# A third store buffer and separate scratch for the squares in the experts' weight conversion of a retention and expert-routing kernel

## The chip, the cores and the metric

The kernel runs on one core of a Trainium2 chip. The core has TensorE for matmuls (with weight loads that the profile lists apart as PEld), VectorE (DVE), ScalarE (ACT), GpSimd (POOL), and SyncE (SP), whose queue issues nearly all DMAs here. The metric is the device time of one execution in microseconds (us), lower being better.

## What is computed

Three layers follow one another on 3072 tokens of width 512. Inputs and outputs are float32.

```python
# retention: per batch and head
state = gamma * state + outer(k[t], v[t])
y[t]  = q[t] @ state / sqrt(D)
# dense layer, d_ff = 2048, with a PReLU
h = x @ w_in
x = (max(h, 0) + alpha * min(h, 0)) @ w_out
# experts: 8 of them, each w1[e] 512x1024 and w2[e] 1024x512, one chosen per token
expert_idx = argmax(normalise(x) @ normalise(expert_emb).T / tau)
out[mask_e] = gate_w[mask_e] * (max(x[mask_e] @ w1[e], 0) @ w2[e])
```

## The kernel before

**Halves.** The large matmuls run on pairs of float16 numbers. A float32 matrix is multiplied by a power of two, its rounded value is the high half, and what is left is the low half; a product then takes three float16 matmuls. `split` does it for a piece of 128x1024: ScalarE writes the high half (an activation with a scale) and VectorE the low half (one scalar_tensor_tensor).

**Order of the work.** Everything is first recorded by a planner (`Plan`) and then issued. The planner knows which instruction reads or writes which bytes of which buffer, adds assumed durations, and from both makes one fixed order for each engine's queue. TensorE's instructions are only put in when their operands are due 1.5 us earlier by its reckoning (`MARGIN`). On the chip each queue runs in that order, and an instruction that must wait holds up all that stand behind it on its engine. A buffer that is free earlier therefore changes two things: what must be waited for, and where the planner puts the instructions.

**The dense layer.** The tokens are taken in 6 blocks of 512. For each block there are 16 steps, 96 in all. A step is `mm1` (12 matmuls of 512 columns into a PSUM bank), then a Relu on ScalarE and three more instructions on ScalarE and VectorE, by which the bank is freed and the halves for the next matmul are made, then `mm2` (12 matmuls). `mm1` is written 2 steps ahead (`LA = 2`). The weights' halves lie in `win` and `wout`, of which 16 chunks of 512 float32 hold the halves; each has two more chunks behind them (`KF + 2`), because the raw weights are read in two chunks further on and shrink forward. These two chunks hold nothing once the dense weights are split. Retention of later tokens and the routing of finished blocks lie between the steps.

**The experts' weights.** While the dense layer runs, the experts' 16 matrices (here called halves 0 to 15, `HALVES`) are read, turned into float16 pairs and written to DRAM (`wsplit`), from where each is loaded when its expert is due. Each goes through in 4 pieces of 128x1024:

- `half_load` reads a piece from DRAM into one of 6 buffers in `stage`.
- `half_scale` lets ScalarE square and sum the 4 pieces (`square_sum`, whose elementwise result goes to scratch and is never read), then a TensorE matmul, `total`, adds the sums over the partitions, and VectorE derives the scale.
- `half_pair` splits a piece into one of the buffers of `out_ring`, stores that to DRAM from SyncE's queue, and reads the piece that is six further on into the buffer that became free.

Before, `out_ring` has two buffers, the last four of `stage`'s 16 float16 chunks, and the squares write their scratch into the same two.

Of the kernel before, what the change touches and what calls it, by code (L numbers as in the profile page):

```python
# [10 lines left out]
F16 = mybir.dt.float16  # L11
# [17 lines left out]
KF = DFF // P  # L29
# [296 lines left out]
def retention_prelu_moe_kernel(ctx: ExitStack, tc, qkv, w_in, w_out, alpha, emb, tau, w1, w2,  # L326
# [14 lines left out]
    def buf(name, shape, dt=F32):  # L341
        return sbuf.tile([P, *shape], dt, name=name, tag=name)
# [12 lines left out]
    def tmp(name, shape, dt=F32, n=2):  # L355
        if name not in small:
            small[name] = Ring([buf(f"{name}_{k}", shape, dt) for k in range(n)])
        return small[name].next()
# [17 lines left out]
    win = buf("win", [KF + 2, 512])  # L376
    wout = buf("wout", [KF + 2, 512])
# [24 lines left out]
    stage16 = stage.rearrange("p c x -> p (c x)").bitcast(F16).rearrange("p (k a x) -> p k a x", k=16, a=2)  # L402
# [22 lines left out]
    def pow2(ss, s, c, hb=None):  # L425

        if hb is None:
            hb = tmp(f"hb{ss.shape[1]}", [ss.shape[1]], I32)
        V.tensor_scalar(out=hb, in0=ss.bitcast(I32), scalar1=0x7F000000, scalar2=1,
                        op0=ALU.bitwise_and, op1=ALU.logical_shift_right)  # L430
        V.tensor_scalar(out=s.bitcast(I32), in0=hb, scalar1=-1, scalar2=c << 23, op0=ALU.mult, op1=ALU.add)
        return hb

    def pow2_inverse(hb, i, c):
        V.tensor_scalar(out=i.bitcast(I32), in0=hb, scalar1=(254 - c) << 23, scalar2=None, op0=ALU.add)

    def total(acc, n):

        ps = m_ring.next()
        T.matmul(out=ps[:, 0:n], lhsT=ones32, rhs=acc, start=True, stop=True)  # L440
        t = tmp("tot", [1])
        V.tensor_reduce(out=t, in_=ps[:, 0:n], axis=AX.X, op=ALU.add)
        return t

    def square_sum(src, acc, junk):
        A.activation(out=junk, in_=src, func=AF.Square, accum_out=acc)
# [268 lines left out]
    iwe = [buf(f"iwe{g}", [E]) for g in range(2)]  # L715
    HALVES = [(e, which) for e in range(E - 1, -1, -1) for which in range(2)]
    raw_ring = Ring([stage[:, 2 * k:2 * k + 2, :].rearrange("p c x -> p (c x)") for k in range(6)])
    out_ring = Ring([stage16[:, 2 * k:2 * k + 2] for k in (6, 7)])
    half_t = {}

    def half_load(p):
# [7 lines left out]
    def half_scale(n):  # L729
        e, which = HALVES[n]  # L730
        acc = tmp("acce", [4])
        for g in range(4):
            square_sum(half_t[n, g], acc[:, g:g + 1], out_ring.bufs[g % 2][:, :, 0, :])
        s = tmp("se", [1])
        c = (C_W1, C_WIDE)[which]
        pow2_inverse(pow2(total(acc, 4), s, c), iwe[which][:, e:e + 1], c)
        half_t[n] = s
# [152 lines left out]
    acc = {}  # L890
# [120 lines left out]
    for i in range(2 * B, NTILE):  # L1011
        c, b = divmod(i, B)
        s = KF * (c - 1) + 3 * b
        early = i < first_late
        if not early:
            k = 2 + int((i - first_late) * 4.5)
            early = k < KF * (c - 2) + 14
            k = min(k, s)
# [9 lines left out]
    for n in range(len(HALVES)):  # L1028
        s = KF + BT + 4 * n
        at(s, half_scale, n)  # L1030
        for g in range(4):
            at(s + 1 + g, half_pair, n, g)
# [4 lines left out]
    for s in range(NS + BT + 12):  # L1037
# [5 lines left out]
        for o in range(BT - 1, -1, -1):  # L1043
            n = s - o
            if n >= NS - KF:
                n = max(s - LAG[o], NS - KF - 1)
# [286 lines left out]
```

## Time and profile before

| what | value |
|---|---|
| median of 3 runs | 1017.08 us |
| lowest and highest | 1011.92 and 1018.13 us |
| the profiled execution's own time | 1014.34 us |
| its span in the profile | 1012.6 us |
| granted TensorE clock, mean over the span | 0.967 of full speed |

The profiled execution is one of its own, 1.7 us longer than the span that the rows below cover, and 2.7 us under the median of the three timed runs. A row's time is measured from the start of the span. "Idle before" is time in which an engine did nothing, put down to what released it last. Nearly all instructions have the line L146, because the planner issues them from one place; the names of the buffers tell them apart. Squares are the rows `stage<-stage`, the scaling activations `stage<-stage,se`, the `total` matmuls `bank<-acce,cst`, reads of raw pieces `stage<-in_w`, stores `wsplit<-stage`.

### The profile page before, as it was taken

The numbers are of one execution on the slowest core, as the hardware profiler recorded it, in microseconds if no ns is written. First come the engines' busy times: TensorE is split into PE (matmuls) and PEld (weight loads), VectorE is DVE, ScalarE is ACT, GpSimd is POOL, SyncE is SP. The second block draws the span as 40 slices with busy tenths as digits, with TensorE's granted clock in tenths as the row PEclk, the third lists the DMA queues.
The fourth block names the chain that finished last, engine by engine and source line by source line (L and its number), as shares of the span: only waits on it lengthen the run. The fifth ranks groups of instructions, "written<-read, shape, count | busy, mean of one in ns | idle before, by whom it ended". The sixth has DMA issues, their size and how long they took to land. (4 is left out here: it accounts for less than half of the span.)

```text
span 1012.6 us, 18929 instructions
## 1 busy us (share of the span) xinstructions
PE 929.1 (92%) x7100; PEld 558.5 (55%) x7100; DVE 569.1 (56%) x1477; ACT 466.2 (46%) x825; POOL 93.3 (9%) x110
## 2 busy tenths in 40 slices
PE   5797889999998999999999899999599999988995
PEld 5774555555544544444444344446476776765763
DVE  4889988488766866686556448638422221221231
ACT  2568865385767777686565557322011010110100
POOL 0000000000100020001000200111311211232010
PEclk9798879999999999999999999999799999999998
DMA  8988623547789866766676655687564599634760
GB/s 298 303 255 268 221 97 112 177 115 196 253 231 231 201 228 221 218 209 209 197 208 187 209 166 161 237 322 176 136 194 115 141 308 319 174 95 114 165 269 23
DMA packets 129823, 201.44 MB, mean 199 GB/s; under 512 B 89726, under 2 KB 90110, under 8 KB 124608
## 3 DMA queue, kind: packets, MB, share of 16 engines
q1 hardware_dynamic: 123168, 179.42, 59.8%
q0 software_dynamic: 6560, 20.77, 6.0%
q8 instruction: 57, 0.93, 0.4%
q14 instruction: 38, 0.31, 0.1%
HBM read 204.59 MB, written 51.14 MB: 253 GB/s over the span
## 5 line engine op out<-in xcount | busy, mean ns | idle before, releaser
L146 PE MATMUL bank<-xT,win 128*128 128x512 f16 (+1 forms) x2208 | 335.5, 308 | 19.9 <-DMA xT<-f_buf 9.4
L146 PEld LDWEIGHTS <-win 128*128 128x128 f16 x2400 | 186.0, 99 | 158.2 <-issue 30.8
L146 PE MATMUL bank<-wout,f_buf 128*128 128x512 f16 x960 | 223.2, 379 | 3.9 <-DVE pay_buf L146 2.8
L146 PEld LDWEIGHTS <-f_buf 128*128 128x128 f16 x960 | 92.2, 99 | 109.3 <-issue 5.8
L146 DVE SCALAR_TENSOR_TENSOR stage<-stage,se 128x1024 f16<-128x1024 f32 x64 | 81.4, 1284 | 40.8 <-ACT stage L146 36.2
L146 DVE SCALAR_TENSOR_TENSOR g<-g,oma,bank 128x512 f32<-128x512 f32 x96 | 71.0, 742 | 41.9 <-ACT g L146 41.5
L146 ACT ACTIVATE st_bd<-bank 128x512 f16<-128x512 f32 x30 | 17.9, 597 | 156.9 <-PE bank L146 121.0
L146 ACT ACTIVATE stage<-stage,se 128x1024 f16<-128x1024 f32 x64 | 71.8, 1142 | 34.1 <-DMA wsplit<-stage 30.9
L146 ACT ACTIVATE stage<-stage 128x1024 f16<-128x1024 f32 x64 | 67.4, 1054 | 34.9 <-DMA wsplit<-stage 30.4
L146 ACT ACTIVATE g<-bank 128x512 f32<-128x512 f32 x96 | 56.2, 588 | 52.5 <-PE bank L146 51.1
L146 DVE SCALAR_TENSOR_TENSOR f_buf<-g,f_buf 128x512 f16<-128x512 f32 x80 | 55.0, 687 | 38.7 <-ACT f_buf L146 37.0
L146 POOL DMA_INDIRECT table<-pay_buf,rposi x24 | 26.2, 1092 | 500.6 <-DVE csum L146 138.0
L146 PEld LDWEIGHTS <-wout 128*128 128x128 f16 x1152 | 65.5, 98 | 7.9 <-issue 5.0
L146 PE MATMUL bank<-xT,wout 128*128 128x128 f16 x1056 | 62.6, 219 | 3.7 <-issue 3.6
L146 ACT ACTIVATE f_buf<-g 128x512 f16<-128x512 f32 x80 | 49.8, 622 | 33.0 <-DVE g L146 32.9
L146 PEld LDWEIGHTS <-st_bd 128*128 128x128 f16 x408 | 39.7, 99 | 45.4 <-issue 1.9
L146 DVE SCALAR_TENSOR_TENSOR st_bd<-bank,st_bd 128x512 f16<-128x512 f32 x34 | 23.5, 690 | 67.1 <-ACT st_bd L146 67.0
L146 DVE TENSOR_SCALAR xT<-bank,f_buf,cqk_sb 128x512 f32<-128x512 f32 x22 | 17.8, 809 | 67.1 <-PE bank L146 67.0
L146 PE MATMUL bank<-win,st_bd 128*128 128x512 f16 x216 | 49.5, 387 | 0.0
L146 POOL DMA_INDIRECT out<-xT,ids x25 | 25.3, 1011 | 217.0 <-DVE xT L146 184.1
L146 PE MATMUL bank<-wout,stage 128*128 128x512 f16 (+1 forms) x200 | 44.6, 375 | 0.0
L146 PE MATMUL bank<-wout,st_bd 128*128 128x512 f16 x192 | 42.7, 379 | 0.0
(249 smaller groups left out, 1129.8 us busy)
## 6 DMA issues: line engine op xcount, KB each, us to landing
win<-wsplit SPq DMA_DIRECT2D x56, 1024.0 KB
wout<-wsplit SPq DMA_DIRECT2D x52, 1024.0 KB
stage<-in_w SPq DMA_DIRECT2D x64, 512.0 KB
wsplit<-stage SPq DMA_DIRECT2D x64, 512.0 KB
qk_buf<-in_qkv SPq DMA_DIRECT2D x15, 768.0 KB
f_buf<-in_w_in SPq DMA_DIRECT2D x12, 512.0 KB
vp_buf<-in_qkv SPq DMA_DIRECT2D x20, 256.0 KB
f_buf<-in_w_out SPq DMA_DIRECT2D x10, 512.0 KB
```

What stands on the lines that cost most here:

```text
L146: call = lambda: fn(**kw)
```

## The change

The third buffer of `out_ring` is the space of two chunks behind `win`'s halves. The squares' scratch moves to the two chunks behind `wout`'s halves, which are cut into two buffers that take turns. The squares no longer touch a buffer that is stored.

```diff
     raw_ring = Ring([stage[:, 2 * k:2 * k + 2, :].rearrange("p c x -> p (c x)") for k in range(6)])
-    out_ring = Ring([stage16[:, 2 * k:2 * k + 2] for k in (6, 7)])
+
+    tail = [w[:, KF:KF + 2].rearrange("p c x -> p (c x)").bitcast(F16) for w in (win, wout)]
+    out_ring = Ring([stage16[:, 2 * k:2 * k + 2] for k in (6, 7)] + [tail[0].rearrange("p (c a x) -> p c a x", c=2, a=2)])
+    junk_ring = Ring([tail[1][:, 1024 * k:1024 * k + 1024].rearrange("p (c x) -> p c x", c=2) for k in range(2)])
     half_t = {}
...
         for g in range(4):
-            square_sum(half_t[n, g], acc[:, g:g + 1], out_ring.bufs[g % 2][:, :, 0, :])
+            square_sum(half_t[n, g], acc[:, g:g + 1], junk_ring.next())
```

No computation is added or taken away. The planner's order changes from the first squares on. Three places follow.

ScalarE, around half 13 (its squares are the rows with `acce_174`; `g_86` and `g_87` are the Relus of the dense steps, `se_175` and `se_176` the scales of the halves before it and of its own). Before:

```order
L146 ACTIVATE stage<-stage,se_175 128x2x512 [waits DMAHW5_49,Activation_49]
L146 ACTIVATE g_87<-bank_94 128x512 [waits DVE_49,PE_49]
L146 ACTIVATE stage,acce_174<-stage 128x2x512 [waits DMAHW7_49,DMAHW6_49]
L146 ACTIVATE stage,acce_174<-stage 128x2x512 [waits DMAHW3_49,Activation_49]
L146 ACTIVATE f_buf<-g_87 128x512 [waits DVE_49]
L146 ACTIVATE stage,acce_174<-stage 128x2x512 [waits DMAHW1_49,DMAHW0_49]
L146 ACTIVATE stage,acce_174<-stage 128x2x512 [waits DMAHW4_49,Activation_49]
L146 ACTIVATE g_86<-bank_93 128x512 [waits PE_49]
L146 ACTIVATE f_buf<-g_86 128x512 [waits DVE_49]
L146 ACTIVATE stage<-stage,se_176 128x2x512 [waits DVE_49]
```

After, in the same place of the work:

```order
L146 ACTIVATE wout,acce_174<-stage 128x1024 [waits DMAHW4_49]
L146 ACTIVATE g_87<-bank_94 128x512 [waits PE_49]
L146 ACTIVATE f_buf<-g_87 128x512 [waits DVE_49]
L146 ACTIVATE wout,acce_174<-stage 128x1024 [waits DMAHW7_49,Activation_49]
L146 ACTIVATE stage<-stage,se_175 128x2x512 [waits DMAHW3_49,DVE_49]
L146 ACTIVATE stage<-stage,se_175 128x2x512 [waits DMAHW5_49]
L146 ACTIVATE g_86<-bank_93 128x512 [waits PE_49,Activation_49]
L146 ACTIVATE win<-stage,se_175 128x2x512 [waits DMAHW0_49]
L146 ACTIVATE f_buf<-g_86 128x512 [waits DVE_49]
L146 ACTIVATE stage<-stage,se_175 128x2x512 [waits DMAHW2_49,Activation_49]
L146 ACTIVATE g_87<-bank_94 128x512 [waits PE_49]
L146 ACTIVATE wout,acce_174<-stage 128x1024 [waits DMAHW3_49]
```

Before, the four squares stand together behind all four scalings of the half before, and two of them have two DMA waits each, one for a piece to arrive and one for a store to end. After, the first two stand ahead of those scalings, and each waits for its piece alone. Over the whole order the last square of half 13 stands behind 76 Relus before and behind 72 after, and its `total` on TensorE behind 77 and 74 `mm1` steps.

ScalarE, where the first squares come in (`ssx`, `ssa`, `spv`, `syv` belong to retention), the difference:

```order
 L146 ACTIVATE v_103<-vp_buf,spv_155 128x512
 L146 ACTIVATE st_y<-st_bd,syv_160 128x512
+L146 ACTIVATE wout,acce_173<-stage 128x1024 [waits DMAHW3_49,DVE_49]
+L146 ACTIVATE wout,acce_173<-stage 128x1024 [waits DMAHW4_49]
 L146 ACTIVATE xh,ssx_130<-bank_95 128x512 [waits DMAHW7_49,PE_49]
 L146 ACTIVATE v_103,ssa_154<-vp_buf 128x512 [waits DMAHW0_49,DVE_49]
 L146 ACTIVATE xh<-bank_95,sx_132 128x512 [waits DVE_49,Activation_49]
 L146 ACTIVATE f_buf<-g_86 128x512
+L146 ACTIVATE wout,acce_173<-stage 128x1024 [waits DMAHW6_49]
 L146 ACTIVATE p_0_101,ssa_154<-vp_buf 128x512 [waits DVE_49]
 L146 ACTIVATE p_1_102,ssa_154<-vp_buf 128x512 [waits DVE_49]
+L146 ACTIVATE wout,acce_173<-stage 128x1024 [waits DMAHW1_49]
```

The squares of half 0 move ahead by some 28 rows, to where retention has ScalarE nearly to itself.

SyncE's queue, around the pieces of half 12 (stores `wsplit`, reads `stage<-in_w`). Before:

```order
L146 DMA wsplit<-stage 128x2048 [waits DMAHW2_49,DVE_49]
L146 DMA stage<-in_w 128x1024 [waits DMAHW3_49]
L146 DMA stage<-in_w 128x1024 [waits DMAHW4_49,DVE_49]
L146 DMA wsplit<-stage 128x2048 [waits DMAHW5_49]
L146 DMA stage<-in_w 128x1024 [waits DMAHW6_49,DVE_49]
L146 DMA wsplit<-stage 128x2048 [waits DMAHW7_49]
```

After:

```order
L146 DMA wsplit<-stage 128x2048 [waits DMAHW2_49,DVE_49]
L146 DMA stage<-in_w 128x1024 [waits DMAHW3_49]
L146 DMA stage<-in_w 128x1024 [waits DMAHW4_49,DVE_49,Activation_49]
L146 DMA wsplit<-win 128x2048 [waits DMAHW5_49]
L146 DMA stage<-in_w 128x1024 [waits DMAHW6_49,DVE_49,Activation_49]
L146 DMA stage<-in_w 128x1024 [waits DMAHW7_49,DVE_49,Activation_49]
L146 DMA wsplit<-win 128x2048 [waits DMAHW0_49]
```

The third store of a half now stands behind the read that needs the fourth piece to be split. TensorE's rows that wait for a DMA are 205 before and after.

## Rows read from the trace of the kernel before

**Rows 1.** The page: busy time, share and instructions of each engine.

```profile
PE 929.1 (92%) x7100; PEld 558.5 (55%) x7100; DVE 569.1 (56%) x1477; ACT 466.2 (46%) x825; POOL 93.3 (9%) x110
```

**Rows 2.** Windows, the stage of the experts' halves; columns as named.

```profile
core 0: us, PE busy (x) PEld busy (x) DVE busy (x) ACT busy (x) POOL busy (x), PEclk, DMA share, GB/s
...
196.00:620.00 424.00, 401.72 (x2400) 200.80 (x2399) 284.67 (x730) 288.23 (x530) 24.79 (x32) 0.99 0.69 205
```

**Rows 3.** Windows of 25 us within that stage, the same columns.

```profile
200.00:225.00 25.00, 25.00 (x185) 14.89 (x184) 19.28 (x49) 20.30 (x43) 0.00 (x0) 1.00 0.45 117
...
325.00:350.00 25.00, 21.78 (x150) 11.64 (x149) 20.18 (x73) 19.74 (x35) 0.00 (x0) 1.00 0.86 185
...
425.00:450.00 25.00, 22.35 (x152) 11.70 (x152) 19.88 (x58) 20.30 (x40) 0.00 (x0) 1.00 0.75 218
```

**Rows 4.** Waits, whole span: us in total, times, longest us.

```profile
ACT stage L146 <- DMA wsplit<-stage: 61.3, 42, 3.9
...
PE bank L146 <- ACT stage L146: 11.7, 10, 3.6
PE bank L146 <- DMA xT<-f_buf: 9.4, 1, 9.4
```

**Rows 5.** Timeline of TensorE: start, duration, instruction [idle before it].

```profile
286.47 0.39 PE L146 MATMUL bank<-acce,cst 128*128 128x4 f32 x2 [1.50 <-ACT stage L146]
...
313.20 0.39 PE L146 MATMUL bank<-acce,cst 128*128 128x4 f32 x2 [1.55 <-DVE rhb L146]
329.80 0.81 PE L146 MATMUL bank<-wout,f_buf 128*128 128x512 f16 x3 [2.39 <-DVE pay_buf L146]
...
370.43 0.39 PE L146 MATMUL bank<-acce,cst 128*128 128x4 f32 x2 [1.83 <-ACT stage L146]
...
424.89 0.39 PE L146 MATMUL bank<-acce,cst 128*128 128x4 f32 x2 [0.62 <-ACT stage L146]
```

**Rows 6.** Timeline around the `total` of half 13.

```profile
576.61 1.06 ACT L146 ACTIVATE stage<-stage 128x1024 f16<-128x1024 f32 x1 [3.12 <-DMA wsplit<-stage]
...
578.99 0.59 PE L146 MATMUL bank<-acce,cst 128*128 128x4 f32 x2 [3.57 <-ACT stage L146]
...
579.44 5.28 PE L146 MATMUL bank<-xT,win 128*128 128x512 f16 x12
...
587.21 2.75 PE L146 MATMUL bank<-xT,win 128*128 128x512 f16 x12
```

**Rows 7.** Windows of 5 us behind it, columns as in rows 2.

```profile
580.00:585.00 5.00, 5.00 (x14) 1.76 (x12) 3.81 (x8) 2.95 (x4) 0.45 (x1) 0.53 0.21 79
595.00:600.00 5.00, 5.00 (x25) 2.29 (x24) 1.44 (x2) 3.41 (x6) 0.00 (x0) 1.00 0.68 216
```

**Rows 8.** Timeline of one piece: scaled, split, stored, and who waits for the store.

```profile
384.97 1.15 ACT L146 ACTIVATE stage<-stage,se 128x1024 f16<-128x1024 f32 x1 [2.31 <-DMA wsplit<-stage]
...
386.15 1.28 DVE L146 SCALAR_TENSOR_TENSOR stage<-stage,se 128x1024 f16<-128x1024 f32 x1 [2.36 <-ACT stage L146]
...
387.46 0.33 SPq L146 DMA_DIRECT2D stage<-in_w  x1
387.84 0.42 SPq L146 DMA_DIRECT2D wsplit<-stage  x1
...
390.95 1.06 ACT L146 ACTIVATE stage<-stage 128x1024 f16<-128x1024 f32 x1 [3.13 <-DMA wsplit<-stage]
```

**Rows 9.** The page, costliest groups: busy us, mean ns | idle before, releaser.

```profile
L146 ACT ACTIVATE stage<-stage,se 128x1024 f16<-128x1024 f32 x64 | 71.8, 1142 | 34.1 <-DMA wsplit<-stage 30.9
L146 ACT ACTIVATE stage<-stage 128x1024 f16<-128x1024 f32 x64 | 67.4, 1054 | 34.9 <-DMA wsplit<-stage 30.4
```

**Rows 10.** Timeline where half 0's fourth square now stands, SyncE's queue and ScalarE.

```profile
182.12 0.33 SPq L146 DMA_DIRECT2D stage<-in_w  x1
...
183.24 0.19 ACT L146 ACTIVATION_READ_ACCUMULATOR p<-vp_buf 128x1 f32 x1
185.85 1.33 ACT L146 ACTIVATE p<-vp_buf,spv 128x512 f16<-128x512 f32 x2 [2.42 <-DVE spv L146]
```

## The prediction, made before the changed kernel ran

> **What bounds the kernel now.** I read the page first. TensorE is busy 92% of the span, ScalarE 46% [rows 1], so a wait of ScalarE is worth only what TensorE loses by it. Then the table of waits: ScalarE waits 61.3 us, 42 times, for stores of the experts' halves, while TensorE waits 11.7 us, 10 times, for a ScalarE write to `stage` [rows 4]. The windows limit the rest: from 196 to 620 us, where the halves are made, TensorE is busy 401.72 of 424 us [rows 2]. The reader should see 61 us of waiting on an engine with slack, and 424.00 - 401.72 = 22.3 us of idle time on the one that counts. No more than these 22.3 us, and what a lowered clock costs, can be won in this stage.
>
> Which instructions lose them is in TensorE's timeline. Ten `total` matmuls wait for the squares, the first at 286.47 us for 1.50 us, the last and worst at 578.99 us for 3.57 us; together they are the 11.7 us of the waits [rows 4 to 6]. An eleventh, at 313.20, waits 1.55 us and is named after VectorE [rows 5]. So 13.2 us of the 22.3 stand before a `total`, and 9.1 us before other instructions, the largest 2.39 us before an `mm2` [rows 5]. The chain at the worst place: ScalarE wants to square the third piece of half 13 at 573.49, stands 3.12 us until a store has left the scratch's buffer, squares two pieces, and only then can TensorE go on [rows 6].
>
> After that gap TensorE's granted clock is 0.53 over 5 us and then 1.00 [rows 7], that is the lower of its two levels, 1.2 GHz, for nearly all of this window. The `mm1` that follows takes 5.28 us where the next takes 2.75 [rows 6]: 2.5 us more, and 0.2 us for the `total` itself (0.59 against 0.39 us, rows 5 and 6). These 2.7 us hang on the 3.57 us gap alone; behind the 2.39 us gap at 329.80 the window's clock is 1.00 [rows 3, 5].
>
> **The change part by part.** *The squares' scratch.* 64 squares of 1.05 us remain as they are [rows 9]; what goes is their wait for stores, 30.4 of ScalarE's 61.3 us [rows 4, 9]. In their place they wait for their piece to arrive. In the new order the read of a piece was requested behind the split six pieces earlier, and I added up ScalarE's own work between that scaling and the square, with the durations of the trace: 6.5 us or more for 56 of the 58 squares, and 3.6 and 5.9 us for two. What must fit in: a scaling starts at 384.97, its split ends at 387.43, read and store go out, and the store has landed by 390.95 [rows 8], so 6.0 us, and the read, issued 0.4 us ahead of the store [rows 8], I expect no later than that. The trace shows no wait for such a read, so its price is bounded by 0 us and by that of a store wait, up to 3.9 us [rows 4]; I take 0 for 56 squares and up to 2.4 us (6.0 - 3.6) for one, which hides unless its `total` is due.
>
> *The third buffer.* A scaling now waits for the store three pieces back. The same sum over the new order gives at least 6.3 us of ScalarE work between the two for 56 of 61 scalings, and 4.7 us (four times) and 5.9 us for the others. Against the 6.0 us this leaves five waits of 0.1 to 1.3 us, some 5 us in place of the 30.9 us of scalings' waits [rows 9]. With two buffers the same sum is 3.5 to 7.9 us for about half of the pieces, which fits the 42 waits seen. TensorE doesn't see these five unless a square stands behind them.
>
> *The place of `total`.* The planner leaves a margin between the last square and `total`, counted in `mm1` steps of TensorE ahead of Relus of ScalarE. Before, 12 halves have one step and 4 have two. After, 4 have one, 10 have two and two have more. This alone would not heal it: the four halves with two steps before waited 0.6 us on average (1.83 and 0.62 us in two of them, rows 5, nothing in the others), those with one 0.9 us. So an upper bound for what stays is 12 x 0.6 + 4 x 0.9 = 10.8 us. The lower bound is 0, because squares come late where ScalarE stood for a store [rows 6], and five sixths or more of those waits go. I take 4 us: the 10.8 us in the proportion of ScalarE's remaining waits (some 10 of 61.3 us with the reads', which gives 1.8), doubled for what the order can't show.
>
> *The clock.* With no gap like the one at 575 us the 2.7 us go in full; if one such gap forms elsewhere they stay.
>
> *The early squares.* Half 0's fourth square now stands behind 183.24 + 0.19 = 183.4 us. Its read went out at 182.12 [rows 10] and has landed 3.1 us after, by the store's figure (387.84 to 390.95, rows 8), at 185.2. It ends at 186.5, 0.6 us behind the time at which the next activation could start [rows 10]. TensorE is busy 25.00 of 25 us in the next window [rows 3], so I cost it at 0, and at 0.6 us if that cover is gone.
>
> *The queue.* On SyncE's queue the third store of a half now stands behind a read that needs the fourth split, so it goes out later by about one split, 1.3 us [rows 8]. Its buffer is wanted only by the second scaling of the next half, with the squares between: nothing. Behind it wait the loads for retention; they stood behind stores before, too.
>
> *The end of the stage.* The `total` of half 15 moves from 87 to 82 `mm1` steps, so the last store comes about 5 steps earlier. Nothing gains: behind 620 us TensorE's longest wait is 9.4 us for a transposed gather [rows 4], which hangs on the last block's routing and not on the halves.
>
> *Sum.* 1014.34 - 13.2 + 4.0 - 2.7 = 1002.4 us on the profiled execution's time. The median of the timed runs is 2.7 us above that, which would make it 1005; the runs scatter over 6 us, so I leave the sum nearly as it is: 1003 us. The 9.1 us of other waits I leave where they are (bounds: all gone, or as much again).
>
> **The rivals.** *The waits stay.* ScalarE loses its stalls but the `total`s are placed just as tightly against squares that now run close behind their reads, and the 10.8 us by steps remain: 13.2 - 10.8 = 2.4 us, and the clock's 2.7, if at all. That is 1009 us, up to 1014 if the clock falls again. For it: half 5, with two steps, still waited 1.83 us [rows 5]. Against it: the stalls in front of the squares go, and in the worst case a stall explains nearly all of the wait [rows 6].
>
> *More than the `total`s.* The 2.39 us before an `mm2` and its like [rows 5] come from the same late ScalarE. If all 22.3 us go, 1014.34 - 22.3 - 2.7 = 989 us. Against it: several follow VectorE's small steps of routing and retention, which don't change.
>
> *Slower: the halves crowd the engines.* The same conversion now ends at step 82 and begins at 23 as before, 59 steps in place of 64. ScalarE's 288.23 of 424 us [rows 2], 68%, become about 74% while it lasts. Windows with ScalarE at 19.74 and 20.30 of 25 us, 79 to 81%, lost 3.2 and 2.7 us of TensorE each [rows 3]; if all 14 windows from 250 to 600 us went that way, it would be 14 x 2.9 = 41 us idle in place of 22.3, and the time 1014.34 + 18.7 - 2.7 = 1030 us. It decides from about 79%, and one window at 81% lost nothing [rows 3]: unlikely.
>
> *It doesn't do what it says.* A wait of TensorE's reads of `win` and `wout` on writes behind their halves would appear as new waits. The order shows none, so only noise would be left: 1014 to 1017 us.
>
> *TensorE has more room than its idle time.* In a stretch with no idle time, 595 to 600 us, 25 matmuls started in 5 us, and weight loads took 2.29 us, 46% [rows 7]; over the stage they take 200.80 of 424 us, 47% [rows 2]. So the stage runs at the rate of its full stretches, by this row, and 22 us is all. If weight loads could fill the stage as they do in the window at 200 us, 14.89 of 25 [rows 3], the 424 us would shrink by a fifth, to about 927 us in all. The Trainium skill's page "Perfetto Trace Analysis", section "Identifying the Most-Contended Engine", says that matmul busy time is a bad measure of headroom and that the weight loads' share should be used; taken as it stands it speaks for that case, and the row of the full stretch speaks against it.
>
> **How the numbers follow.** The forecast, 1003 us (998 to 1008), gets 0.50; the waits stay, 0.28; more than the `total`s, 0.10; crowding, 0.08; nothing done, 0.02; more room, 0.02. The range of 990 to 1015 us holds all but crowding and the last two cases and the ends of the others, and takes in the bounds of 0 and 10.8 us on what stays. About 1% is what a measurement of this kernel can tell from no change; against 1017.08 that is below 1007 or above 1027. Faster by over 1%: most of the forecast (0.43), the larger gain and the last case (0.12) and a little of the second (0.02), 0.57. Slower: crowding and scatter, 0.09. Within: 0.34.
>
> **What would show it.** In the changed kernel's waits, ScalarE's wait for stores should be 5 to 20 us in place of 61.3, with no wait of over 10 us in all for reads. TensorE's waits before `total` should be at most 5 us, and no window between 250 and 620 us should show a clock below 1.00. TensorE's idle time from 196 to 620 us should be about 13 us. The prediction is wrong if the `total`s wait as before with ScalarE's stalls gone (the second case), or if new gaps before `mm1`, `mm2` or retention take what the `total`s gave.

## The result, and the profile after

The changed kernel takes 988.02 us, the median of four runs (986.31 to 989.68), beside 1016.94 us for the kernel before (four runs, 1011.92 to 1018.13). The ratio is 0.973, with a 95% interval of 0.969 to 0.977. Ratios here and below are taken over the runs in the usual, faster state, so a ratio need not be the quotient of two medians. The forecast was 1003 us in a range of 990 to 1015: the sign was right, the gain about twice the one forecast. The profiled execution took 989.28 us, its span 987.5 us.

The page of the kernel after: the engines, then ScalarE's two groups of the experts' halves. The squares' scratch now carries the name `wout`, and a third of the scalings write to `win`.

```profile
PE 926.0 (94%) x7100; PEld 560.5 (57%) x7100; DVE 570.0 (58%) x1477; ACT 464.7 (47%) x825; POOL 91.7 (9%) x110
...
L146 ACT ACTIVATE wout<-stage 128x1024 f16<-128x1024 f32 x64 | 67.3, 1052 | 36.9 <-DMA stage<-in_w 36.3
...
L146 ACT ACTIVATE stage<-stage,se 128x1024 f16<-128x1024 f32 x43 | 48.8, 1139 | 10.5 <-DMA wsplit<-stage 6.6
```

The work is the same as before, [rows 1, 9], within 3.1 us on any engine. What ScalarE waits for has changed: stores 61.3 us before, 6.6 now (and 2.1 for those from `win`), but 36.3 us for reads of raw pieces, for which no wait was named before. The table of waits after, whole span, shows how often and the longest:

```profile
ACT wout L146 <- DMA stage<-in_w: 36.3, 32, 3.6
...
PE bank L146 <- DMA xT<-f_buf: 7.7, 1, 7.7
...
ACT stage L146 <- DMA wsplit<-stage: 6.6, 4, 2.2
```

The windows that answer to [rows 2, 3]:

```profile
196.00:620.00 424.00, 420.50 (x2559) 212.99 (x2557) 307.72 (x818) 298.50 (x554) 25.59 (x35) 1.00 0.72 215
325.00:350.00 25.00, 24.81 (x194) 13.74 (x193) 22.76 (x79) 18.47 (x33) 0.00 (x0) 1.00 0.74 219
425.00:450.00 25.00, 25.00 (x188) 13.16 (x186) 22.31 (x94) 20.11 (x42) 0.98 (x1) 1.00 0.84 256
```

TensorE was idle for 22.28 us of this stage before and for 424.00 - 420.50 = 3.50 us now. All of it lies ahead of 600 us in both, so the windows below end there. What is left of TensorE's waits from 196 to 600 us:

```profile
PE bank L146 <- DVE roh L146: 2.7, 1, 2.7
PE bank L146 <- DVE xh L146: 0.6, 1, 0.6
PE bank L146 <- DVE st_bd L146: 0.2, 1, 0.2
```

No `total` waits any more: the ten waits for the squares [rows 4 to 6] are gone, and so is the eleventh [rows 5]. Of the other waits one is left, `st_bd`, 0.5 us before and 0.2 now; the two named after `roh` and `xh` are new.

**Where the 25.1 us went.** The span fell from 1012.6 to 987.5 us. In the stage the idle time fell by 22.28 - 3.50 = 18.8 us. TensorE's busy time fell by 3.0 us (929.08 to 926.05, summed over windows): what the clock took around the slow `mm1` of [rows 6] is gone (2.7 us), and a smaller loss of that kind has come (1.4 us, last section). The remaining 1.7 us are a balance of other matmuls that wasn't followed up; part of it runs the other way, since the clock stood lower late in this profile than before (0.83 from 880 to 910 us, against 0.94 from 905 to 935 us). Outside the stage some 3.3 us are left, of which the transposed gather's wait is 9.4 - 7.7 = 1.7 us. I don't put that down to the change: the same wait was 9.6 us in a second profile of this kernel, and between 4.3 and 10.3 us over all runs.

### The profile page after: what moved, and what is told of

Same layout as the page of the kernel before. It is cut to its first block, busy times and chain, and to the rows that moved or that the text cites. A ratio compares the mean times of both kernels' runs of the same rounds, so it can differ in the third digit from the quotient of the medians.

```text
span 987.5 us, 18911 instructions
## 1 busy us (share of the span) xinstructions
PE 926.0 (94%) x7100; PEld 560.5 (57%) x7100; DVE 570.0 (58%) x1477; ACT 464.7 (47%) x825; POOL 91.7 (9%) x110
## 5 line engine op out<-in xcount | busy, mean ns | idle before, releaser
L146 PE MATMUL bank<-xT,win 128*128 128x512 f16 (+1 forms) x2208 | 333.7, 308 | 18.2 <-DVE g L146 8.1
L146 ACT ACTIVATE wout<-stage 128x1024 f16<-128x1024 f32 x64 | 67.3, 1052 | 36.9 <-DMA stage<-in_w 36.3
L146 PEld LDWEIGHTS <-st_bd 128*128 128x128 f16 x408 | 39.9, 100 | 47.5 <-issue 4.7
L146 DVE SCALAR_TENSOR_TENSOR stage<-stage,se 128x1024 f16<-128x1024 f32 x43 | 55.1, 1281 | 8.3 <-ACT stage L146 8.1
L146 ACT ACTIVATE stage<-stage,se 128x1024 f16<-128x1024 f32 x43 | 48.8, 1139 | 10.5 <-DMA wsplit<-stage 6.6
L146 PEld LDWEIGHTS <-x2T_buf 128*128 128x128 f16 x384 | 27.0, 98 | 28.2 <-issue 2.8
```

Of the source, the lines that this page charges most:

```text
L146: call = lambda: fn(**kw)
```

## The experiments

Theory S: ScalarE's stalls for stores were the whole cost, those in front of squares by way of the `total`s, those in front of scalings by way of VectorE, which stands behind them. Rival O: the new order did it, with two `mm1` steps of slack for most `total`s. Rival K (from the waits after): ScalarE's waits for reads are harmless only because of that slack. The experiments separate the two halves of the change, the order from the buffers, and the slack from the stalls. Ratios are to the kernel before on the same chip, because its median was 1013, 1002 and 1019 us in the three sets below. The times that were expected of each experiment go by an earlier chip than the one it ran on, so they are compared as gains where that matters.

First the whole, so that each experiment can be read against it. "Stalls" is ScalarE's waiting for stores and reads, in front of squares and of scalings; "idle" is TensorE's from 196 to 600 us, in front of `total`s and of all else. Each row is read from a profile of its kernel; that of "before" is the one of [rows 1 to 10], because no set below has a profile of it.

| kernel | ratio (95%) | stalls: squares | stalls: scalings | idle: `total`s | idle: others |
|---|---|---|---|---|---|
| before | 1 | 30.4 | 30.9 | 13.2 | 9.1 |
| after, again | 0.975 (0.972 to 0.978) | 38.8 | 9.1 | 0 | 4.3 |
| scratch alone | 0.977 (0.974 to 0.980) | 39.9 | 18.2 | 0 | 6.9 |
| third buffer alone | 0.990 (0.987 to 0.994) | 39.3 | 17.5 | 9.8 | 1.4 |
| old order, new buffers | 0.973 and 0.971 | 0 | 0 | 0 | 0 |
| old order, scratch alone | 0.978 (0.973 to 0.982) | 0 | 36.8 | 0.6 | 4.5 |
| old buffers, late `total`s | 1.005 (1.001 to 1.009) | 42.4 | 32.9 | 0 | 12.8 |
| after, early `total`s | 0.987 (0.983 to 0.992) | 32.0 | 12.7 | 14.9 | 0.1 |
| after, reads reckoned late | 0.966 (0.962 to 0.970) | 3.1 | 2.2 | 0 | 0 |
| after, five read buffers | 0.977 (0.971 to 0.982) | 54.7 | 9.0 | 0.2 | 8.8 |

**1. The squares' scratch alone.** Two stored buffers as before, the scratch behind `wout`.

```diff
-out_ring = Ring([stage16[:, 2 * k:2 * k + 2] for k in (6, 7)] + [tail[0]...])
+out_ring = Ring([stage16[:, 2 * k:2 * k + 2] for k in (6, 7)])
```

> Only the squares' scratch moves; the ring of stored buffers stays at two. Both theories below let the scratch carry the change, and say 988 to 994 us, TensorE's waits at the total matmuls under 3 us. If the third buffer carries it, 1003 to 1012 us. ScalarE should wait for stores about 30 us, by the scalings alone.

It gave 989.32 us against 1013.15, nearly the whole gain. ScalarE waits 18.2 us for stores, where about 30 were expected.

```profile
196.00:600.00 404.00, 397.10 (x2405) 201.55 (x2405) 288.21 (x739) 289.13 (x535) 23.02 (x32) 1.00 0.75 220
```

The idle time is 404.00 - 397.10 = 6.9 us, none of it at a `total`. But the planner has given this kernel a new order as well, so it can't tell S from O.

**2. The third buffer alone.** The squares write into the first two stored buffers again.

```diff
-square_sum(half_t[n, g], acc[:, g:g + 1], junk_ring.next())
+square_sum(half_t[n, g], acc[:, g:g + 1], out_ring.bufs[g % 2][:, :, 0, :])
```

> Only the third buffer; the squares still write into the first two stored buffers. If the scratch carries the change: 1008 to 1015 us, with 8 us or more of waits at the totals. If the third buffer does: 990 to 998 us.

It gave 1002.73 us against 1013.15, between the two forecasts. The squares' stalls remain, 39.3 us, and the `total`s wait 9.8 us; the scalings' stalls fall to 17.5 us, and the other idle time to 1.4. One more `total` waits 1.65 us at 604.78 us, behind the window. This kernel, too, has an order of its own.

```profile
196.00:600.00 404.00, 392.83 (x2378) 197.42 (x2377) 279.31 (x722) 283.57 (x523) 26.35 (x32) 1.00 0.71 215
```

**3. The new buffers in the old order.** The planner is shown the old buffers, so that every queue has the order of before, and the instructions use the new ones. This is what separates S from O: the slack is one step for most `total`s.

```diff
+old_ring = Ring([stage16[:, 2 * k:2 * k + 2] for k in (6, 7)])
...
+plan.old = {"out": old_ring.bufs[g % 2][:, :, 0, :]}
 square_sum(half_t[n, g], acc[:, g:g + 1], junk_ring.next())
...
+o, old = out_ring.next(), old_ring.next()
+plan.old = {"out": old[:, :, 0]}
+A.activation(out=o[:, :, 0], in_=two(src), func=AF.Copy, scale=s)
...
```

The low half and the store are treated in the same way. The lines of `Plan` by which it records the buffer in `plan.old` are left out here.

> The instructions use the new buffers, but the planner is shown the old ones, so that every queue has the order of the kernel before. Theory S (ScalarE's stalls for stores were the cost, the place of the instructions is secondary): 989 to 997 us, waits at the totals under 4 us. Theory O (the new order, with squares early and two steps between the last square and its total, is what helps): 1005 to 1014 us, with 8 us or more of waits at the totals although the store waits are gone.

It gave 985.4 us against 1013.15 (0.973, 0.970 to 0.977), less than even theory S had said. In the trace TensorE's 7100 matmuls and SyncE's 427 DMAs follow one another as in the kernel before. TensorE doesn't wait once in the stage, nor ScalarE for any store or read:

```profile
196.00:600.00 404.00, 404.00 (x2456) 205.38 (x2455) 292.93 (x765) 295.16 (x547) 25.99 (x32) 1.00 0.73 219
```

So O falls: with the order of before the whole gain is there.

**4. Late `total`s with the old buffers.** The rival's other side: each `total` stands 4.5 us behind its last square by the planner's reckoning, in place of 1.5, which gives two steps to most halves.

```diff
...
+plan.margin = 4500
+tot = total(acc, 4)
+plan.margin = plan.MARGIN
-pow2_inverse(pow2(total(acc, 4), s, c), iwe[which][:, e:e + 1], c)
+pow2_inverse(pow2(tot, s, c), iwe[which][:, e:e + 1], c)
```

> The kernel before with its two shared buffers; the planner puts each total at least 4.5 us behind its reckoned last square in place of 1.5, which gives two steps for 11 halves in place of 4. Theory S: the store waits stay, so do the waits in front of other instructions, 9 us; at best the totals' 13 us go: 1000 to 1008 us. Theory O: most of the gain with no change to a buffer, 990 to 1000 us.

It gave 1020.82 us against 1013.15, no gain, so neither forecast was met. The `total`s no longer wait, but the other idle time of the stage grows from 9.1 to 12.8 us:

```profile
196.00:600.00 404.00, 391.21 (x2364) 197.84 (x2363) 269.84 (x706) 272.18 (x506) 21.39 (x29) 1.00 0.67 197
```

And the conversion lasts longer: its last store goes out at 663.5 us instead of 641.7, and TensorE's waits behind 600 us now include these, which before were 1.1 us for `x2T_buf` and none for `rlg`:

```profile
PE bank L147 <- DMA x2T_buf<-pay_buf: 12.1, 3, 7.7
PE bank L147 <- DVE rlg L147: 8.2, 1, 8.2
```

So slack at the `total`s took 9.5 us of idle time out of the stage, and the kernel was no faster: the loss came back behind it, where the conversion ends later. Why the end grows just these waits wasn't tried.

**5 to 8, on one chip.** The kernel after and the third experiment once more, to set the orders side by side:

> The changed kernel once more, to stand beside the next run on the same chip: 986 to 990 us.

> The new buffers in the old order once more. If the old order, with squares late, spares ScalarE the waits for reads and with them what TensorE still loses: 2 to 5 us under the changed kernel. If those waits cost nothing, the two are the same within 2 us.

After took 977.87 us (six runs, 976.78 to 978.98; the 986 to 990 us expected were the first chip's), the old order with the new buffers 973.77 (six runs, 973.17 to 977.26; ratio 0.971, 0.968 to 0.975). The idle time is 4.3 and 0 us. The new order is thus not the source of the gain but costs about 4 us of it.

The seventh kernel takes the third one and gives it two stored buffers, so that only the scratch differs from before:

```diff
-out_ring = Ring([stage16[:, 2 * k:2 * k + 2] for k in (6, 7)] + [tail[0]...])
+out_ring = Ring([stage16[:, 2 * k:2 * k + 2] for k in (6, 7)])   # order of before
```

> The old order and two stored buffers; only the squares' scratch is apart. The order of every queue is that of the kernel before, so this takes away the squares' half of the store waits alone (30.4 of 61.3 us) and leaves the scalings' half. If the totals' waits come from the squares' stalls: the 13 us at the totals go, some of the other 9 us stay, 992 to 1000 us. If it is the sum of ScalarE's stalls that counts, about half of the gain: 998 to 1004 us.

It gave 979.72 us against 1002.25. As a gain that is 22.5 us. The 992 to 1000 us of the first case are 13 to 25 us under the 1013 to 1017 us of the kernel before on the earlier chips, the 998 to 1004 us of the second case 9 to 19, so the first case came. All of ScalarE's stalls stand in front of scalings now, and TensorE's waits are mostly named after VectorE. The waits of ScalarE over the span, and the windows:

```profile
ACT stage L147 <- DMA wsplit<-stage: 36.8, 27, 3.7
```

```profile
196.00:600.00 404.00, 398.89 (x2421) 202.26 (x2419) 287.96 (x749) 291.40 (x539) 23.00 (x32) 1.00 0.73 217
```

One `total` waits, for 0.6 us; the other 4.5 us of idle time lie elsewhere, half of the 9.1 before. At one and the same order the squares' stalls are thus worth 12.6 us of `total`s and 4.6 us of other waits, and the scalings' the last 5.1 us.

The eighth tests K: the kernel after, with each `total` as early as the planner can put it.

```diff
...
+plan.margin = -1500
+plan.bias = -40000.0
+tot = total(acc, 4)
+plan.margin, plan.bias = plan.MARGIN, 0.0
```

> The changed kernel, with each total put into TensorE's queue as soon as the planner allows and 1.5 us ahead of its reckoned last square; on average 1.6 steps lie between them in place of 2.1, none for three halves. ScalarE keeps its waits for reads (36 us). If it is the two steps that make these waits harmless: waits at the totals of 5 to 15 us and 993 to 1003 us. If the waits for reads are too short to matter anyway: 986 to 991 us.

It gave 991.59 us against 977.87 for after on the same chip. The stalls are no longer than after's, yet nine `total`s wait for 14.9 us, two of them named after VectorE's `xh` and one after its `vp_buf`. TensorE from 354 us, the worst of them:

```profile
354.22 0.59 PE L147 MATMUL bank<-acce,cst 128*128 128x4 f32 x2 [3.63 <-ACT wout L147]
354.68 2.72 PE L147 MATMUL bank<-wout,f_buf 128*128 128x512 f16 x6
```

That fits K: waits for reads much like those that cost no `total` anything in after stand beside 14.9 us of waits where 11 of the 16 halves have one step or none. In front of the six `total`s that wait for a square, 10.7 us in all, ScalarE had stood 10.1 us for reads among the squares of the last 8 us. But a `total` set 1.5 us ahead of its reckoned last square could wait by itself, and no run has early `total`s without the waits for reads. K is argued, not shown.

**9 and 10, on one chip: the reads.** If the reads' late landing is what the new order didn't allow for, then a planner that reckons them 3 us later should put the squares where the pieces have landed:

```diff
+late = 3000.0 if kw["out"].tensor.name.startswith("stage") else 0.0
-return 60.0, (1150.0 if "transpose" in method else 1000.0), ...
+return 60.0, late + (1150.0 if "transpose" in method else 1000.0), ...
```

> The changed kernel, with its buffers; the planner reckons 3 us more until a read into the stage buffers lands, so squares stand further behind their reads. If ScalarE's waits for reads (36 to 39 us) come from reads that land later than the planner reckons, they fall under 15 us. If they still cost TensorE its last 3 to 4 us of the stage, the ratio to the kernel before comes to that of the old order with new buffers, 0.971; if not, it stays at 0.975.

And one read buffer fewer, by which each read is requested a piece later:

```diff
-raw_ring = Ring([... for k in range(6)])
+raw_ring = Ring([... for k in range(5)])   # half_load(... + 5), five first loads
```

> The changed kernel with 5 buffers for the pieces that are read in place of 6, so each read goes out one piece later. ScalarE's waits for reads rise from 36 to 50 us or more. If ScalarE's waits are paid by how much they are in all: 993 us or more on a chip where the kernel before takes 1015 (ratio 0.980 or more). If two steps ahead of the totals cover them: within 0.3% of the changed kernel's ratio, 0.973 to 0.978.

With reads reckoned late the time is 982.15 us against 1019.0, the lowest ratio of all, 0.966 where 0.971 was expected: its interval lies under that of after (0.972 to 0.978) and overlaps that of the old order (0.968 to 0.975). After itself wasn't run on this chip. No wait of TensorE is left in the stage, and of ScalarE's for reads 3.1 us:

```profile
196.00:600.00 404.00, 404.00 (x2459) 205.17 (x2458) 300.46 (x779) 293.61 (x541) 26.56 (x32) 1.00 0.75 223
```

```profile
ACT wout L146 <- DMA stage<-in_w: 3.1, 3, 1.5
```

TensorE had no idle time in the stage in the old order either, so what lies between 0.966 and 0.971 comes from elsewhere, and wasn't looked for.

With five buffers it is 994.45 us on the same chip. The ratio, 0.977, lies in the range of the second forecast, but its interval, 0.971 to 0.982, also takes in the 0.980 of the first. The trace says more: the reads' waits grow to 54.7 us and the idle time to 9.0, of which only 0.2 stands before a `total`. So the steps of slack cover the `total`s here, and not the instructions behind VectorE.

## Why the prediction was right in sign and wrong in size

**What bounds the kernel** was read rightly: the 22.3 us of idle time in the stage and a lowered clock were all there was to win there, and in the third and ninth kernels exactly that is won, 404.00 of 404.

**The squares' scratch: the `total`s' 13.2 us.** Right in mechanism, and more so than forecast. I took 4 us to stay, between 0 and 10.8. They were 0, and 0.6 us in the old order with the scratch alone, where most halves keep one step. So the 10.8 us by steps, which took the 0.6 and 0.9 us that halves waited before as what a step of slack can't hide, were stalls as well, and "doubled for what the order can't show" had no ground.

**"The 9.1 us of other waits I leave where they are": the step that failed.** 3.5 us of such waits stand in the new kernel, and only 0.2 of them at a place that waited before. I held against their going that several follow VectorE's small steps, which don't change. What delayed those steps did change. The timeline of the kernel before, ScalarE and VectorE ahead of the 2.39 us wait at 329.80 [rows 5]:

```profile
325.46 1.15 ACT L146 ACTIVATE stage<-stage,se 128x1024 f16<-128x1024 f32 x1 [2.86 <-DMA wsplit<-stage]
326.51 0.58 ACT L146 ACTIVATE pay_buf<-bank 128x512 f16<-128x512 f32 x1
326.64 1.28 DVE L146 SCALAR_TENSOR_TENSOR stage<-stage,se 128x1024 f16<-128x1024 f32 x1 [2.66 <-ACT stage L146]
...
327.84 0.15 DVE L146 TENSOR_SCALAR rhb<-rss 128x1 int32<-128x1 int32 x1
...
328.99 0.75 DVE L146 SCALAR_TENSOR_TENSOR pay_buf<-bank,rsc,pay_buf 128x512 f16<-128x512 f32 x1 [0.22 <-ACT pay_buf L146]
```

A scaling stands 2.86 us for a store, the activation behind it comes late, and VectorE, next in line with that piece's low half, stands 2.66 us. Routing's steps queue behind both, and TensorE's wait bears the name of the last, `pay_buf`. The rows were there to be read before the run; I stopped at the releaser's name. That the stalls were the cause is shown by the third kernel, in which the order is the same and these waits are 0, and by the seventh, where the scalings' stalls alone leave 4.5 us.

**The clock.** The 2.7 us went as forecast, but 1.4 us came back behind a new gap, where I had forecast no window below 1.00 between 250 and 620 us. **The end**, put at nothing, is in the 3.3 us outside the stage; half of that scatters from run to run (first section), the rest stays open.

**The sum, forecast against measured:** 4.0 us at the `total`s that didn't stay, 9.1 - 3.5 = 5.6 us of others, 3.3 us outside the stage, and 0.3 us of busy time (3.0 instead of 2.7) make 13.2 us. The profiled execution was 1002.4 - 989.3 = 13.1 us under the sum.

**The reads: a wrong term that cost nothing at first sight.** I took 0 us for 56 squares and up to 2.4 for one; it is 36.3 us in 32 waits. One piece in the timeline after, from its scaling to the square that uses its buffer next, and the `total` behind that:

```profile
464.58 1.13 ACT L146 ACTIVATE stage<-stage,se 128x1024 f16<-128x1024 f32 x1
465.75 1.28 DVE L146 SCALAR_TENSOR_TENSOR stage<-stage,se 128x1024 f16<-128x1024 f32 x1 [1.86 <-ACT stage L146]
...
467.06 0.33 SPq L146 DMA_DIRECT2D stage<-in_w  x1
...
467.44 0.42 SPq L146 DMA_DIRECT2D wsplit<-stage  x1
471.90 1.06 ACT L146 ACTIVATE wout<-stage 128x1024 f16<-128x1024 f32 x1 [3.55 <-DMA stage<-in_w]
...
473.34 0.28 PE L146 MATMUL bank<-acce,cst 128*128 128x4 f32 x2
```

This square starts 471.90 - 464.58 = 7.3 us behind the scaling, and 4.8 us behind the read's issue. I had 6.0 us for the first, with the read landing no later than a store, 3.1 us behind its issue [rows 8]. So the read lands later than a store of the same 512 KB in [rows 8], from which I had its time. The 32 squares that waited start 3.6 to 8.0 us behind the issue of their read, 5.9 in the median; whether it is the direction or the traffic around it wasn't tried. With reads reckoned 3 us later (ninth kernel) the waits fall from 36 to 3.1 us. It was hidden, as the forecast's escape clause had it, because no `total` was due: here it starts without a wait.

**The early squares and the queue**, both put at nothing: TensorE's busy time ahead of 196 us is 163.44 us before and 163.79 after, so nothing is lost there, and no wait for a load behind the later stores has come.

**The third buffer.** Five waits of some 5 us in all were forecast for the scalings; six of 8.7 us came. At a fixed order it is worth 979.72 - 973.77 = 6.0 us on one chip, where I had credited it with nothing that TensorE sees.

**The place of `total`.** Forecast as no cure by itself, and the fourth kernel bears that out. In the new order it seems to matter, where 36 us of read waits may otherwise be felt (the eighth kernel, which fits this without showing it). I had not joined the two.

**The rivals.** "More than the `total`s", all 22.3 us and the clock's 2.7 for 989 us, was the case that came, with a chance of 0.10 and the right mechanism: the same late ScalarE. That its 989 us were met to 0.3 us in the profiled execution is luck in part: 3.5 us of idle time were left and 1.4 us of the clock came back, and 3.3 us outside the stage, of which it said nothing, made up for most of that. "The waits stay" is refuted by the seventh kernel, with the `total`s where they were. Crowding did not come: in the new kernel ScalarE is busy 292.47 of 404 us, 72%, and in the window at 425 us, 20.11 of 25 us or 80%, TensorE loses nothing, where I had put the turning point at 79%. "TensorE has more room": in the third kernel weight loads take 205.38 of 404 us, 51%, with TensorE busy for all of it, and two different orders end at that same figure; no run has more over this stretch. By the Trainium skill, page "Perfetto Trace Analysis", section "Identifying the Most-Contended Engine", the measure is not the busy share of the matmuls but the share of the weight loads, beside MFU (the matmul work done as a share of the peak). Here 51% was what a stretch without idle time shows, so the share of the weight loads by itself would have promised room that no run found; MFU wasn't worked out.

## What to carry to other kernels

A wait that bears the name of an engine with time to spare is read one step further back: look at what stood in front of its queue, and count the waits of everything behind the same stall as one loss. Stalls and slack are looked at apart: a us of ScalarE's stall cost TensorE 0.36 us before and 0.08 after, in another order. So a changed buffer is judged with the order held fixed, and then a planner is told what its transfers take. The landing time of a transfer is taken from a row of its own kind, and where there is none it keeps wide bounds.

## What the hardware showed unexpectedly

**The length of a gap doesn't tell whether the clock falls.** TensorE after, and the chain into it:

```profile
525.41 1.15 ACT L146 ACTIVATE stage<-stage,se 128x1024 f16<-128x1024 f32 x1 [1.74 <-DMA wsplit<-stage]
...
526.59 1.28 DVE L146 SCALAR_TENSOR_TENSOR stage<-stage,se 128x1024 f16<-128x1024 f32 x1 [0.43 <-ACT stage L146]
527.79 0.16 DVE L146 COPY rlg<-bank 128x8 f32<-128x8 f32 x1
...
529.32 0.17 PE L146 MATMUL bank<-roh,cst 128*128 128x8 f16 x1 [2.71 <-DVE roh L146]
...
529.75 4.11 PE L146 MATMUL bank<-xT,win 128*128 128x512 f16 x12
533.70 2.75 PE L146 MATMUL bank<-wout,f_buf 128*128 128x512 f16 x12
```

```profile
530.00:535.00 5.00, 5.00 (x19) 1.98 (x18) 2.41 (x15) 4.88 (x15) 0.98 (x1) 0.75 0.99 395
```

The last large wait of the new kernel is again a scaling that stalls for a store, 1.74 us, with VectorE's split and the routing's steps behind it. TensorE stands 2.71 us, and its granted clock is 0.75 over the 5 us from 530, between its two levels of 1.2 and 2.4 GHz, so at the lower for part of them. Twelve matmuls take 4.11 us instead of 2.75, and 1.4 us are lost beside the gap. Before, the gap of 2.39 us at 329.80 left the clock at 1.00 [rows 3, 5], and that of 3.57 us brought it to 0.53 [rows 6, 7].

It would be easy to read a shortest harmful gap out of this. Two other profiles forbid it. At the same place of the work, with the same matmuls ahead of the gap (an `mm2`, then two of 8 columns), the second profile of the kernel after and the one with five read buffers show:

```profile
530.68 0.17 PE L146 MATMUL bank<-roh,cst 128*128 128x8 f16 x1 [2.47 <-DVE roh L146]
...
531.08 2.75 PE L146 MATMUL bank<-xT,win 128*128 128x512 f16 x12
```

```profile
536.25 0.17 PE L146 MATMUL bank<-roh,cst 128*128 128x8 f16 x1 [1.75 <-DVE roh L146]
...
536.65 4.44 PE L146 MATMUL bank<-xT,win 128*128 128x512 f16 x12
```

The gap of 2.47 us costs nothing behind it: the granted clock is 1.00 from 530 to 535 us. The gap of 1.75 us is followed by 0.68 from 535 to 540 us and by twelve matmuls in 4.44 us. What decides beside the length isn't shown.

**One kernel on different chips.** The kernel before had medians of 1013, 1002 and 1019 us in the three sets, and 1017 in the first comparison. That spread of 1.5 to 1.7% is over half of the gain studied, which is why no times of different sets are compared here. Whether the chip makes it or something else isn't shown. The two profiles of the kernel after show where it sits: of the 11.9 us between their spans (987.5 and 975.6), all lie behind 600 us, where TensorE is busy for 361.8 and 354.7 us and idle for 25.7 and 20.9. In the first its granted clock is 0.83 from 880 to 910 us, in the second 1.00 from 868 to 898 us, at the same distance from the end.
